# A complex-decay linear attention and a softplus layer on one core: paced loads, low halves by identity products, 48-column key-value products, a new plan

## The chip, the cores and the metric
One core of a Trainium2 chip runs the whole program. The metric is the device time of one execution in microseconds (us); lower is better.

## The reference, cut to what matters
Batch 4, 8 heads, 768 steps, head width 48; tokens of width 384 go through a layer of inner width 2048.

```python
scale = np.minimum(mag, 0.999) / (mag + 1e-06)      # mag = |a|, complex decay per step and row
for t in range(S):
    new_re = ar * S_re - ai * S_im
    new_im = ar * S_im + ai * S_re
    S_re, S_im = (new_re + einsum('bhd,bhe->bhde', k[:, :, t], v[:, :, t]), new_im)
    y[:, :, t] = einsum('bhd,bhde->bhe', q[:, :, t], S_re)
x = y.transpose(0, 2, 1, 3).reshape(B * S, H * D)
h = x @ w_in                                         # (3072, 384) @ (384, 2048)
g = np.maximum(h, 0.0) + np.log1p(np.exp(-np.abs(h)))
out = g @ w_out                                      # (2048, 384)
```

## The kernel before, in words
The steps are cut into 24 chunks of 128 steps of one batch. Four chunks, one of each batch, make a group of 512 tokens, so there are six groups. For the first group each chunk is a slice of its own (four slices); later slices hold two chunks.

For a slice, `pre` turns the decay into running sums of its logarithm and of its angle and multiplies q and k by the resulting exponentials, sines and cosines (VectorE and ScalarE, some 20 instructions a slice; for the first group the running sums are TensorE products with a triangle, L583). The last two steps, L654 and L656, are the slice's tail. `chunk` then moves the turned q and k into another layout by four DMAs from SBUF to SBUF (L702, L706; tile `qk`), multiplies them (scores, L748), masks them (L752), multiplies with v (L784, tile `y`) and, from the second group on, adds the state's part (L781). It also transposes k (L721) and adds the key-value products to the state (L810), which need the tiles `v` and `vo`. The tokens `y` go into `xt` as a high half (L793) and a low half (L794), so that products of float32r tiles keep float32's precision: three such products, high by high, high by low and low by high, stand for one.

`moe` runs the layer for a group: for each of 16 f blocks nine products into `h` (L846), the softplus on ScalarE and VectorE, and nine products into three accumulators `o` (L882); in the first group the second product takes w_out as plain float32 (L879, three products a block). The weights arrive as pairs of 32-bit words in eight blocks each of w_in and w_out (L388, 768 KB a load). VectorE puts the words together (L398, L401, L405); for a w_in block ScalarE then rounds the high half (L412) and VectorE subtracts it for the low half (L415).

All instructions are tasks of a planner. It simulates the five engines and one DMA server with the costs written at each task and with keys from a table `K`, and so fixes the order of each engine. On the chip, each engine runs its list in order and waits on semaphores. SP issues all loads and moves, so a DMA that waits holds back all that stand behind it. Where the simulated TensorE has nothing to do ahead of the layer's first second product, the planner puts filler products in its list (L908, results unused).

## Time and profile before

| | us |
|---|---|
| median of three runs | 579.37 (579.27 to 582.35) |
| the profiled execution | 580.82 |
| its span, first to last instruction | 579.1 |
| TensorE busy | 551.1 |
| VectorE busy | 430.9 |
| ScalarE busy | 426.8 |
| first of the layer's products (L846) starts at | 66.33 |

Read it from both ends. TensorE is busy for nearly the whole span, yet until the layer starts a part of that is filler. So the profile has two parts: a head, up to some 66 to 72 us, in which the first group's tokens are made, and a long rest in which the products of the layer follow each other with the later groups' attention between them. A float32 product appears as two instructions in the trace. Names of engines in rows: PE is TensorE, DVE is VectorE, ACT is ScalarE, SPq is the queue of SyncE.

### The profile page before, as it was taken

What the parts mean: (1) busy time and instruction counts of PE and PEld (TensorE: products, weight loads), DVE (VectorE), ACT (ScalarE), POOL (GpSimd) and SP (SyncE); (2) the same over time, 40 slices, a digit from 0 to 9 for tenths busy, and PEclk for the clock granted to TensorE, in tenths of its full rate; (3) what the DMA queues carried; (4) which work ended last, traced back from release to release, by engine and by line L of the source; (5) the groups of instructions that cost most, each with busy time, mean ns of one, the idle gap of its engine ahead of it and who ended that gap; (6) DMA issues with size and microseconds to landing.
All of it is one profiled execution on the core that took longest, in us unless ns stands there. A gap on an engine that the chain in (4) does not pass through costs nothing.

```text
span 579.1 us, 14114 instructions
## 1 busy us (share of the span) xinstructions
PE 551.1 (95%) x5952; PEld 439.9 (76%) x5952; DVE 430.9 (74%) x669; ACT 426.8 (74%) x756; POOL 3.8 (1%) x23
## 2 busy tenths in 40 slices
PE   0998899999999999999999999999999999999995
PEld 0997766576677888888888888888888878888883
DVE  6696899999897999988688767776966543544442
ACT  7972597868589798785977847958949899854442
POOL 2000000000000000000000000000000000000000
PEclk9998999999999999999999999999999999999998
DMA  8879920162644414464251532412247975120002
GB/s 316 351 213 278 406 96 0 35 184 58 164 148 110 141 33 103 149 166 142 65 168 48 118 125 70 117 35 102 69 126 236 306 236 184 42 55 0 1 0 60
DMA packets 44262, 76.09 MB, mean 131 GB/s; under 512 B 3744, under 2 KB 29344, under 8 KB 44192
## 3 DMA queue, kind: packets, MB, share of 16 engines
q1 hardware_dynamic: 44192, 75.12, 42.7%
q8 instruction: 48, 0.79, 0.6%
q14 instruction: 22, 0.18, 0.1%
HBM read 51.51 MB, written 4.72 MB: 97 GB/s over the span
## 4 chain that ended last, share of the span: by engine, by line
PE 82%; ACT 7%; DVE 4%; DMA 3%; issue 2%; SPq 0%; ACTq 0%; DVEq 0%
PE h L846 31%; PE o L882 25%; PE o L879 7%; PE att L748 4%; PE o L908 3%; PE att L810 3%; PE att L781 3%; PE att L784 2%; PE att L721 2%; ACT seen L460 1%; DMA seen<-w_in_dram 1%; DMA x<-dense_dram 1%; ACT lt L852 1%; ACT seen L459 1%; DMA seen<-w_out_dram 1%
## 5 line engine op out<-in xcount | busy, mean ns | idle before, releaser
L846 PE MATMUL h<-xt,wi 128*128 128x512 f32 x864 | 220.1, 402 | 1.5 <-DVE lt L862 1.2
L846 PEld LDWEIGHTS h<-xt,wi 128*128 128x128 f32 x864 | 159.6, 188 | 42.6 <-issue 2.9
L882 PE MATMUL o<-gh,wo 128*128 128x512 f32 x480 | 161.3, 397 | 0.0
L862 DVE SCALAR_TENSOR_TENSOR lt<-h,lt 128x512 f32<-128x512 f32 x80 | 54.6, 689 | 97.4 <-ACT lt L853 96.8
L882 PEld LDWEIGHTS o<-gh,wo 128*128 128x128 f32 x480 | 90.1, 188 | 21.1 <-issue 0.6
L851 ACT ACTIVATE lt<-h 128x512 f32<-128x512 f32 x96 | 56.2, 594 | 67.2 <-PE h L846 62.8
L882 PE MATMUL o<-gl,wo 128*128 128x512 f32 x240 | 94.1, 392 | 0.0
L853 ACT ACTIVATE lt<-lt,fixed 128x512 f32<-128x512 f32 x96 | 68.5, 721 | 1.5
L852 ACT ACTIVATE lt<-lt 128x512 f32<-128x512 f32 x96 | 59.9, 632 | 1.6
L866 DVE TENSOR_TENSOR gl<-lt,gh 128x512 fp32r<-128x512 f32 x80 | 54.6, 689 | 3.7 <-ACT gh L865 1.2
L882 PEld LDWEIGHTS o<-gl,wo 128*128 128x128 f32 x240 | 45.1, 188 | 9.7 <-DVE gl L866 0.2
L879 PE MATMUL o<-gf,raw_wo 128*128 128x512 f32 x96 | 43.5, 594 | 0.0
L966 ACT ACT_TABLE_LOAD x30 | 38.5, 1283 | 0.5
L562 DVE TENSOR_TENSOR_SCAN t<-hold,t 128x384 f32<-128x384 uint8 x40 | 36.1, 945 | 0.7
L752 DVE TENSOR_TENSOR a<-att,mask 128x512 f32<-128x512 f32 x48 | 31.4, 684 | 6.7 <-PE att L748 3.8
L748 PE MATMUL att<-qk 96*32 96x96 f32 (+3 forms) x1536 | 33.5, 236 | 1.9 <-issue 1.9
L748 PEld LDWEIGHTS att<-qk 96*32 96x32 f32 x1536 | 30.3, 111 | 6.1 <-issue 4.5
L879 PEld LDWEIGHTS o<-gf,raw_wo 128*128 128x128 f32 x96 | 17.9, 190 | 17.7 <-issue 16.3
L908 PE MATMUL o<-ident 128*128 128x128 f32 x198 | 27.6, 293 | 0.0
L908 PEld LDWEIGHTS o<-ident 128*128 128x128 f32 x198 | 25.6, 206 | 0.9 <-issue 0.6
L864 DVE TENSOR_SCALAR gh<-lt 128x512 fp32r<-128x512 f32 x52 | 22.0, 425 | 3.7
L865 ACT ACTIVATE gh<-lt 128x512 fp32r<-128x512 f32 x28 | 17.2, 626 | 8.7 <-DVE lt L862 8.6
(95 smaller groups left out, 694.4 us busy)
## 6 DMA issues: line engine op xcount, KB each, us to landing
x<-dense_dram SPq DMA_DIRECT2D x20, 768.0 KB, 5.8
qk<-x SPq DMA_DIRECT2D x48, 288.0 KB, 4.2
raw_wo<-w_out_dram SPq DMA_DIRECT2D x8, 768.0 KB, 8.1
raw_wi<-w_in_dram SPq DMA_DIRECT2D x8, 768.0 KB, 10.3
seen<-w_in_dram SPq DMA_DIRECT2D x16, 384.0 KB, 4.2
seen<-w_out_dram SPq DMA_DIRECT2D x16, 384.0 KB, 4.9
v<-vpad_dram SPq DMA_DIRECT2D x24, 224.0 KB, 2.8
qk<-x SPq DMA_DIRECT2D x48, 96.0 KB, 3.7
```

Of the source, the lines that this page charges most:

```text
L562: V.tensor_tensor_scan(out()[:, s], self.hold, inc()[:, s], 0.0, ALU.mult, ALU.add)
L748: PE.matmul(psc()[QT * u : QT * (u + 1), hh * P + f : (hh + 1) * P], q[:, h, CH + f : CH + f + QT], q[:, h, f:CH], start=True, stop=True)
L846: PE.matmul(h()[:, :n], w()[:, q, i, fs], xt()[:, x, i], start=k == 0, stop=k == 3 * NI - 1)
L851: add("ACT", a1(n) - 0.04, lambda: A.activation(tv(), h(), AF.Abs), k, r=[h], w=[t])
L852: add("ACT", a1(n), lambda: A.activation(tv(), tv(), AF.Exp, scale=-1.0), k, w=[t], tab="log")
L853: add("ACT", a1(n, 1), lambda: A.activation(tv(), tv(), AF.Ln, bias=self.one), k, w=[t], tab="log")
L862: add("DVE", d1(n), lambda: V.scalar_tensor_tensor(tv(), h(), 0.0, tv(), ALU.max, ALU.add), k, r=[h], w=[t])
L866: add("DVE", d1(n), lambda: V.tensor_tensor(gl(), tv(), gh().bitcast(F32), ALU.subtract), k, r=[t, gh], w=[gl])
L879: PE.matmul(acc[m]()[:, :n], v, gt[0](), start=f == 0, stop=f == NF - 1)
L882: PE.matmul(acc[m]()[:, :n], w()[:, wq, f % 2, ms], x(), start=f == 0 and q == 0, stop=f == NF - 1 and q == 2)
L908: self.nc.tensor.matmul(self.acc0[0]()[:, :P], self.ident, x, start=True, stop=True)
L966: nc.scalar.preload_act_table_set(TABLES[table])
```

## The change
1. Loads of weights, x, v and vo that the plan starts after 10 us get one more wait: for the ScalarE or VectorE instruction that, in the plan, was the last to end before the load's start.
2. The low halves of w_in blocks 0 to 3 are made by TensorE: identity times the value (float32) plus a negated identity times the high half, in two pieces of 384 columns, in PSUM; ScalarE or VectorE copies each piece out. Before, VectorE subtracted (L415).
3. The first group's tokens get their low half by one product of the negated identity with the high half, added onto `y` in PSUM, and a copy. Before, VectorE subtracted (L794). The negated identity lies in the room of w_out block 4.
4. The key-value products of even heads have 48 columns where they had 64; copies and additions of the state have 384 columns where they had 448. GpSimd clears the four states at the start.
5. Three in ten of each run of fillers, all but the first runs, are left out. ScalarE may take the sign step of the angle (L621). The planner's DMA server is faster for loads (400 KB per us after 0.5, where it was 330 after 0.65) and slower for the moves of q and k; a transpose costs 0.32 where it cost 0.25. All keys in `K` are new, so the whole order is new.

The diff, without the table `K` and with some bookkeeping left out (the loads of x, v and vo get `.pace = True` as the weight load does; `minus` is the negated identity):

```diff
+NLOW = 4
 NAT = {"i": 0, "o": 8}
 FILL = 0.2233
+KEEP = 0.7
+PACED = 10.0
...
                 if e == "SP":
-                    dma_free = max(dma_free, now + dur + 0.65) + t.nbytes / 330e3
-                    t.end = dma_free + 2.0
+                    dma_free = max(dma_free, now + dur + 0.5) + t.nbytes / 400e3
+                    t.end = dma_free + 1.7
...
-        return out
+        return self.thin(out)
+
+    def thin(self, out):
+        runs, run = [], []
+        for t in out:
+            if t.eng == "PE":
+                if t.idx < 0:
+                    run.append(t)
+                elif run:
+                    runs.append(run)
+                    run = []
+        drop = set()
+        for run in runs:
+            if run[0].start > runs[0][0].start + 2 * self.WIN:
+                drop.update(run[math.ceil(KEEP * len(run)) :])
+        return [t for t in out if t not in drop]
...
+        minus = self.minus = Buf(self.wpool, f"wo{TRIB - 1}", [P, 2 * NI * WCOL], F32R, "minus")
...
+        for sp in self.state:
+            add("POOL", 0.5, lambda sp=sp: G.memset(sp(), 0.0), -1e5, w=[sp])
...
+        add("DVE", 0.2, lambda: V.tensor_scalar(minus()[:, :P], self.ident, -1.0, None, ALU.mult), -1e5, w=[minus])
...
-            add("SP", 0.45, load, k - K["rlead"], w=[raw], nbytes=n * self.wwords * 4 * P)
+            add("SP", 0.45, load, k - K["rlead"], w=[raw], nbytes=n * self.wwords * 4 * P).pace = True
...
-                add("DVE", d1(n), lambda: V.tensor_tensor(
-                    flat(fin, 1), bits()[:, :n].bitcast(F32), flat(fin, 0).bitcast(F32), ALU.subtract),
-                    k, r=[bits, (fin, 0)], w=[(fin, 1)])
+                if kind == "o" or b >= NLOW:
...
+                    return
+                for z in range(2):
+                    ps = Buf(self.ps, "h", [P, 512], F32, f"low{b}_{z}", 2)
+                    h = slice(z * n // 2, (z + 1) * n // 2)
+
+                    def differ(ps=ps, h=h):
+                        nc.tensor.matmul(ps()[:, : n // 2], self.ident, bits()[:, h].bitcast(F32), start=True, stop=False)
+                        nc.tensor.matmul(ps()[:, : n // 2], self.minus()[:, :P], flat(fin, 0)[:, h], start=False, stop=True)
+
+                    add("PE", 0.86, differ, k, r=[bits, (fin, 0), self.minus], w=[ps])
+                    x = add("ACT", a1(n // 2), lambda ps=ps, h=h: A.activation(flat(fin, 1)[:, h], ps()[:, : n // 2], AF.Copy),
+                            k, r=[ps], w=[(fin, 1)])
+                    x.alt["DVE"] = (d1(n // 2), lambda ps=ps, h=h: V.tensor_copy(flat(fin, 1)[:, h], ps()[:, : n // 2]))
...
         def fold():
-            add("DVE", d2(W), lambda: V.tensor_scalar(
+            x = add("DVE", d2(W), lambda: V.tensor_scalar(
...
+            x.alt["ACT"] = (a1(W), lambda: A.activation(v4(), v3(), AF.Abs))
...
-        add("DVE", d1(DM), lambda: V.tensor_tensor(
-            xt()[:, 1, :, off : off + CH], y3(), hi().bitcast(F32), ALU.subtract),
-            at(), r=[y, (xt, (gc, 0))], w=[(xt, (gc, 1))])
+        lo = lambda: xt()[:, 1, :, off : off + CH]
+        if first:
+            add("PE", 0.19, lambda: PE.matmul(y3(), self.minus()[:, :P], hi(), start=False, stop=True, skip_group_check=True), at(), r=[(xt, (gc, 0)), self.minus], w=[y])
+            x = add("ACT", a1(DM) - 0.05, lambda: A.activation(lo(), y3(), AF.Copy), at(), r=[y], w=[(xt, (gc, 1))])
+            x.alt["DVE"] = (d1(DM), lambda: V.tensor_copy(lo(), y3()))
...
-                    s = slice(c0, c0 + (D if h % 2 else VP - D))
+                    s = slice(c0, c0 + D)
...
+            def reals(t):
+                a = t()[: 2 * D, :VW]
+                return bass.AP(a.tensor, a.offset, [a.ap[0], (VP, H // 2), (VP - D, 2), (1, D)])
...
+            done = []
             for t in self.plan.order(lambda: self.filler(self.ident), self.opener, self.gate):
...
                 t.fn()
+                ins = nc.cur_bb.bb.instructions[-1]
+                if t.eng in ("ACT", "DVE"):
+                    done.append((t.end, ins))
+                elif t.pace and t.start > PACED:
+                    after = max((x for x in done[-60:] if x[0] <= t.start), key=lambda x: x[0])
+                    self.tc.add_manual_dep(ins, after[1].name, mybir.DependencyInfo(
+                        mybir.DependencyClass.Sync, mybir.DependencyReason.DATA), reason="pace")
```

## Rows read from the trace of the kernel before

**Rows 1.** Page part 1: busy time, share of the span and instructions of each engine.
```profile
PE 551.1 (95%) x5952; PEld 439.9 (76%) x5952; DVE 430.9 (74%) x669; ACT 426.8 (74%) x756; POOL 3.8 (1%) x23
```

**Rows 2.** Stages: length; busy time of each engine; clock granted; DMA share; GB/s.
```profile
30.00:46.00 16.00, 16.00 (x365) 14.96 (x363) 15.33 (x27) 12.64 (x27) 0.00 (x0) 1.00 0.86 236
46.00:66.30 20.30, 15.74 (x357) 14.46 (x357) 13.67 (x21) 4.50 (x7) 0.00 (x0) 0.92 0.99 332
...
72.00:140.00 68.00, 68.00 (x556) 44.16 (x555) 66.78 (x94) 54.01 (x87) 0.00 (x0) 1.00 0.25 76
...
440.00:480.00 40.00, 39.56 (x454) 32.15 (x453) 19.83 (x34) 36.70 (x88) 0.00 (x0) 1.00 0.83 253
```

**Rows 3.** Page part 5, the fillers: line, count, busy us, mean ns of one, idle before.
```profile
L908 PE MATMUL o<-ident 128*128 128x128 f32 x198 | 27.6, 293 | 0.0
```

**Rows 4.** Timeline of PE, 45 to 67 us: start, us, line, count, idle before.
```profile
48.71 0.25 PE L810 MATMUL att<-v,kt 128*32 128x64 f32 x3 [2.69 <-issue]
...
48.91 1.81 PE L748 MATMUL att<-qk 96*32 96x32 f32 x62
...
54.61 1.31 PE L748 MATMUL att<-qk 96*32 96x128 f32 x64
...
58.51 0.66 PE L748 MATMUL att<-qk 96*32 96x128 f32 x22
61.04 1.01 PE L748 MATMUL att<-qk 96*32 96x32 f32 x42 [1.87 <-issue]
61.98 1.83 PE L908 MATMUL o<-ident 128*128 128x128 f32 x14
63.73 1.08 PE L784 MATMUL y<-a,v 128*32 128x128 f32 x32
...
66.33 4.43 PE L846 MATMUL h<-xt,wi 128*128 128x512 f32 x18
```

**Rows 5.** Timeline of DVE, same stretch.
```profile
42.01 0.96 DVE L656 TENSOR_TENSOR x<-x,t 128x768 f32<-128x768 f32 x1
...
61.52 1.29 DVE L752 TENSOR_TENSOR a<-att,mask 128x512 f32<-128x512 f32 x2 [1.68 <-PE att L748]
```

**Rows 6.** DMA issues, median us to landing: 26 to 66, then 100 to 440.
```profile
raw_wi<-w_in_dram SPq DMA_DIRECT2D x5, 768.0 KB, 11.0
...
qk<-x SPq DMA_DIRECT2D x8, 288.0 KB, 7.5
...
v<-vpad_dram SPq DMA_DIRECT2D x3, 224.0 KB, 12.5
...
qk<-x SPq DMA_DIRECT2D x36, 288.0 KB, 4.1
v<-vpad_dram SPq DMA_DIRECT2D x17, 224.0 KB, 2.7
```

**Rows 7.** Waits of SP's queue, 0 to 80: us in total, times, longest.
```profile
SPq L702 <- DVE x L656: 14.5, 1, 14.5
```

**Rows 8.** DVE by line, 0 to 72; then ACT's tokens by line.
```profile
L415 DVE TENSOR_TENSOR wi<-bits_wi,wi 128x768 fp32r<-128x768 f32 x3 | 2.9, 950 | 0.0
L794 DVE TENSOR_TENSOR xt<-y,xt 128x384 fp32r<-128x384 f32 x4 | 2.2, 558 | 2.2 <-ACT xt L793 2.2
...
L793 ACT ACTIVATE xt<-y x4: 491/491/492, 42.6 to 64.9; 128x384 fp32r<-128x384 f32 x4
```

**Rows 9.** Chain of waits in order of time: start, us, line, count.
```profile
72.32 2.09 PE h L846 x9
74.41 2.57 PE o L879 x6
```

**Rows 10.** Timeline of PE: key-value products of one chunk.
```profile
31.16 0.29 PE L810 MATMUL att<-v,kt 128*32 128x64 f32 x6
31.27 0.26 PE L810 MATMUL att<-vo,kt 128*32 128x48 f32 x6
31.36 0.29 PE L810 MATMUL att<-v,kt 128*32 128x64 f32 x6
```

More of the change, by code (lines that the diff above doesn't have):

```diff
@@ L88 @@
 class Task:
-    __slots__ = ("eng", "dur", "fn", "key", "idx", "deps", "outs", "bufs", "tab", "nbytes", "left", "ready", "end", "alt", "mode")
+    __slots__ = ("eng", "dur", "fn", "key", "idx", "deps", "outs", "bufs", "tab", "nbytes", "left", "ready", "start", "end", "alt", "mode", "pace")
     def __init__(self, eng, dur, fn, key, idx, tab, nbytes, mode=0):
@@ L93, in __init__ @@
         self.eng, self.dur, self.fn, self.key, self.idx, self.tab, self.nbytes = eng, dur, fn, key, idx, tab, nbytes
-        self.deps, self.outs, self.bufs, self.end = set(), [], [], 0.0
+        self.deps, self.outs, self.bufs, self.start, self.end, self.pace = set(), [], [], 0.0, 0.0, False
         self.alt = {}
@@ L241, in order @@
                     t = Task("PE", FILL, filler, 0, -1, None, 0)
+                    t.start = now
                     free[e] = now + self.array(now, t.dur + (self.SWITCH[0] if mode else 0.0))
@@ L271, in order @@
                 free[e] = now + dur
-                t.end = now + dur
+                t.start, t.end = now, now + dur
                 if e == "SP":
-                    dma_free = max(dma_free, now + dur + 0.65) + t.nbytes / 330e3
-                    t.end = dma_free + 2.0
+                    dma_free = max(dma_free, now + dur + 0.5) + t.nbytes / 400e3
+                    t.end = dma_free + 1.7
                 ends.append((t.end, t))
@@ L527, in pre @@
                 region(j), self.dense[:, base + 2 * j * W : base + 2 * (j + 1) * W].rearrange("p (c n) -> p c n", c=m)),
-                k + 0.1 * j, w=w, nbytes=8 * W * P)
+                k + 0.1 * j, w=w, nbytes=8 * W * P).pace = True
         for c in range(m):
@@ L532, in pre @@
             add("SP", 0.45, lambda vt=vt, gc=gc: nc.sync.dma_start(vt()[:, :VW], self.vpad[:, gc, :VW]),
-                K["chunk"][gc] - K["vlead"], w=[vt], nbytes=4 * VW * P)
+                K["chunk"][gc] - K["vlead"], w=[vt], nbytes=4 * VW * P).pace = True
             if not last:
@@ L536, in pre @@
                 add("SP", 0.45, lambda vo=vo, gc=gc: nc.sync.dma_start(vo()[:, :VO], self.vpad[:, gc, VW:]),
-                    K["state"][gc] - K["vlead"], w=[vo], nbytes=4 * VO * P)
+                    K["state"][gc] - K["vlead"], w=[vo], nbytes=4 * VO * P).pace = True
         add("ACT", a1(W), lambda: A.activation(v1(), re(), AF.Ln), at(), r=ra, w=[t1], tab="log")
@@ L587, in sums, with keep @@
             return ps, v, t
-        def keep(j, c, ps, v, key):
+        def keep(j, c, ps, v, key, last=()):
             f = car[j]
@@ L592, in keep @@
             add("DVE", 0.07, lambda: V.tensor_copy(
-                f().rearrange("p (b i) -> p b i", b=2)[:, q], n3(v())[:, :, CH - 1]), key, r=[ps], w=[(f, q)])
+                f().rearrange("p (b i) -> p b i", b=2)[:, q], n3(v())[:, :, CH - 1]), key, r=[ps], w=[(f, q), *last])
         part = lambda z, c: z if first else (z, c)
@@ L605, in pre @@
                         at(), r=[lb], w=ca if first else [(x, (c, 0))], tab="log")
-                keep(0, c, lb, vl, at())
+                keep(0, c, lb, vl, at(), [lb])
         else:
@@ L709, in chunk @@
         for y in range(2):
-            add("SP", 0.62, lambda y=y: heads(y), at(), r=rs, w=[(room, y)], nbytes=2 * D * NI * 1024)
+            add("SP", 0.62, lambda y=y: heads(y), at(), r=rs, w=[(room, y)], nbytes=3 * D * NI * 1024)
         for y in range(2):
-            add("SP", 0.62 if y else 1.4, lambda y=y: shared(y), at(), r=rs, w=[(room, 2 + y)], nbytes=2 * D * 1024)
+            add("SP", 0.62 if y else 1.4, lambda y=y: shared(y), at(), r=rs, w=[(room, 2 + y)], nbytes=3 * D * 1024)
         if not last:
@@ L731, in evac @@
                                  p3[:, :, 2 * D :].rearrange("p i (y r) -> p i y r", y=2), AF.Copy)
-                add("PE", 0.25, trans, at("state"), r=[q for q in rs if q[1] != (zc, 1 - j)], w=[pst])
+                add("PE", 0.32, trans, at("state"), r=[q for q in rs if q[1] != (zc, 1 - j)], w=[pst])
                 add("ACT", 0.43, evac, at("state"), r=[pst], w=[(kt, j)])
@@ L771, in ymm @@
         def ymm():
-            yy, q, v = y(), qk(), vt()
+            yy, v = y(), vt()
             def o(G):
@@ L777, in ymm @@
             if not first:
-                s = sp()
+                s, q = sp(), qk()
                 for G, h, co, prim in sched:
@@ L785, in ymm @@
                           start=first and prim and G < 4, stop=not prim)
-        add("PE", 0.9 if first else 1.78, ymm, at(), r=[room, vt] + am + ([] if first else [sp]), w=[y], mode=1)
+        add("PE", 0.9 if first else 1.78, ymm, at(), r=[vt] + am + ([] if first else [room, sp]), w=[y], mode=1)
         off = b * CH
@@ L1172 @@
+        7019.775, 6367.468, -1885.414, 3338.459, 627.569, 6737.113,
     ],
     "moe": [
[L1174 removed]
+        48.696, 119.345, 228.067, 305.249, 451.499, 6921.054,
     ],
     "step": [
[L1177 removed]
+        4.749, 7.163, 4.63, 7.188, 17.603, 4004.219,
     ],
[L1179 to L1184 removed]
@@ L1185 @@
-    "mpen": 2.176,
-    "altpen": 0.035,
-    "tpen": 0.597,
+    "seen": 423.345,
+    "seenstep": 10.777,
+    "rlead": 308.396,
+    "xlead": -1254.94,
+    "vlead": -1611.951,
+    "backlog": 1.427,
+    "mpen": 5.895,
+    "altpen": 0.69,
+    "tpen": 9.883,
     "table": 1.3,
     "nudge": {
[28 rows of a table removed]
[136 rows of a table added]
     },
```

56 lines of the change are left out of this document (26 added, 30 removed), and 164 rows, old and new, of the table K.

## The prediction

> **What bounds the kernel now.** I read the page's first part, then the busy time by stages, and only then single engines. TensorE is busy 551.1 us of a span of 579.1 [rows 1], so 28.0 us are left as idle, and of the busy time 27.6 us are fillers that compute nothing [rows 3]. The other 523.5 us are work. A shorter run can therefore come from three places: from the 27.6 + 28.0 = 55.6 us that are no work, from fewer columns on TensorE, or from a clock that is higher where it is low.
>
> The stages say where the 55.6 us lie. From 72 to 140 us TensorE is busy throughout and VectorE 66.78 of 68 us; even in the busy stretch from 440 to 480 TensorE is idle only 0.44 us of 40 [rows 2]. All fillers, and nearly all idle time other than the drain at the end, lie ahead of the layer's first product at 66.33 us [rows 3, 4]. So the head is what can be shortened, and each microsecond by which the layer starts earlier shortens the run by one, as long as TensorE stays fed afterwards.
>
> What ends the head? The tail of the last of the four slices ends at 42.01 + 0.96 = 42.97 us [rows 5], yet the last scores end only at 61.04 + 1.01 = 62.05 [rows 4]. In between ScalarE is busy 4.50 of 20.3 us and VectorE 13.67, but the DMA engines 0.99 of their time [rows 2]. A move of q and k takes 7.5 us there against 4.1 later, a v load 12.5 against 2.7, and a w_in load 11.0 [rows 6]. So this stretch is one of transfers that stand in each other's way: weights wanted much later are carried beside moves wanted now. Two breaks show it: TensorE stops 2.69 us before a key-value product, and 1.87 us in the middle of one group of scores (22 instructions before, 42 after it) [rows 4]. The profile names no releaser for either; both lie in the stretch of full DMA engines, which is all that the rows say.
>
> **The change part by part.** The profiled execution took 580.82 us for its span of 579.1, 1.45 us above the median of 579.37. I sum against 580.82 and take 1.45 off at the end.
>
> *Pace and new order in the head.* The loads keep their bytes and number; they are issued later, so the moves of q and k and the v loads find freer engines. What the full engines cost on the way to the layer is the two breaks, 2.69 + 1.87 = 4.56 us, and the longer move of the last chunk, 7.5 - 4.1 = 3.4 us: together 8.0 us. The ends: nothing, if the engines turn out to bind; and at most what VectorE allows. It works 13.67 us in that stretch [rows 2], from which the change takes three L415 (2.9 us) and four L794 (2.2 us) [rows 8], leaving 8.6 us, so the layer can't start before 46 + 8.6 = 54.6, a gain of 11.7 us. (The bare chain allows a little more: 42.97 + 4.1 for the move, 1.31 scores, 1.29 mask, 1.08 y, 0.49 and 0.56 for the halves gives 51.8 [rows 4 to 6, 8].) I take 8.0, since VectorE ran 15.33 of 16 us in the stretch ahead [rows 2] and could fill the shorter one almost as densely. The added wait stands on SP: behind a held load queue the moves of q and k, for which the scores wait, and the next x and v loads, for which ScalarE's first step of a slice and the products with v wait. In the head that is the slower rival below. After it I price the wait at nothing, as the DMA engines are at 0.25 of their time from 72 to 140 us [rows 2] and loads land in 2.7 to 4.1 us [rows 6]; if that cover is gone, it is the +4.6 of the rest below.
>
> *Fewer fillers.* A run of 14 fillers takes 1.75 us (61.98 to 63.73) [rows 4]. The mask for the last y ends at 61.52 + 1.29 = 62.81 [rows 5], so y starts 0.9 us late behind fillers. Three in ten of 14 are 0.5 us, and there is one such run before y and one before the layer: a gain of 1.0, between 0 and 1.8 (both waits wholly).
>
> *Low halves of w_in.* Nine float32r products of 512 columns take 2.09 us, 0.232 each; six instructions, three float32 products, take 2.57 us, 0.857 each [rows 9]. Two pieces of 384 columns are three quarters of that: 0.643 + 0.174 = 0.82 us each, and eight pieces make 6.5 us more on TensorE. What lies under fillers costs nothing; what comes after the layer's start costs in full. Three L415 lay before 72 us [rows 8] with the start at 66.33; with a start 8 us earlier I put two blocks in the head and two after it: 3.3 us, ends 0 and 6.5. The eight copies (like L793, 0.49 us for 384 columns [rows 8]) go to ScalarE, which has 15.8 us free between 46 and 66; if it has none, VectorE gets them back and its relief is gone.
>
> *Low half of the tokens.* Four products of 0.174 us, three under fillers; the last chunk's path gets 0.17 + 0.49 us in place of 0.56: +0.1.
>
> *Key-value products.* A 64-column group takes 31.27 - 31.16 = 0.11 us to the next, a 48-column one 0.09 [rows 10]. Four heads of each of 16 chunks after the head: 4 x 16 x 0.02 = -1.3 us; the first four chunks' share is under fillers. The smaller copies of the state save some 0.05 us of an engine off the path each. Clearing the states on GpSimd, the negated identity on VectorE (0.2 us by the planner) and the sign step on ScalarE lie beside other work and count for nothing; without that cover they would be some tenths at the start.
>
> *The rest of the order.* From 72 us on there is little to win: I take 0, from -0.4 (the idle time of the one stretch shown) to +4.6 (the two breaks over again at another place).
>
> Sum: -8.0 - 1.0 + 3.3 + 0.1 - 1.3 = -6.9, so 573.9 for an execution like the profiled one, and 572.5 for the median.
>
> **The rivals.** *The head is shorter still* (0.14). VectorE's bound is met and all low halves find room under fillers: -11.7 - 1.0 + 0.1 - 1.3 = -13.9, so 565.5. For it: ScalarE is mostly idle there. Against: the low halves need fillers that a short head no longer has.
>
> *The engines bind* (0.16). The transfers are hidden anyway: VectorE, which is nearly full before 46 and after 72 us [rows 2], sets when the words of w_in and w_out are ready, and the layer, started early, waits for them. Then 2 us of the 8.0 stay and the low halves are paid: -2.0 + 3.3 + 0.1 - 1.3 = +0.1, so 579.5, the same. For it: 66.78 of 68 us. Against: the change relieves just this engine.
>
> *The clock falls* (0.06). After the break of 2.69 us, 62 score instructions took 1.81 us where 64 took 1.31 [rows 4], and the granted clock is 0.92 of 2.4 GHz over the stretch [rows 2], so part of it ran at 1.2. With three in ten fillers gone the gaps are longer. If the last scores (1.31), y (1.08) and the first 18 products of the layer (4.43) ran at half clock, that is 6.8 us, and -6.9 becomes 579.3. Against: the runs keep seven in ten. The Trainium skill speaks against this part of the change: "TensorE: Matmul & The Clock Gate", "HAM oscillation", says that an array left idle too long falls back to half its clock and the next burst starts slow, and advises to keep it busy. The trace agrees in that one place.
>
> *The pace holds back the moves* (0.14), the slower end. SP works strictly in order: before, it once waited 14.5 us for the first tail [rows 7] with all loads behind it. If a held load ahead of a move waits for an instruction that runs later on the chip than in the plan, the moves behind it are late, and with them the weights; transfers that fill 0.99 of the stretch [rows 2] can't catch up. A w_in load takes 11.0 us where a fresh v load takes 2.7 [rows 6], so one weight load late by 8 us undoes the gain of 8.0 and adds as much again: +8.0 - 1.0 + 3.3 + 0.1 - 1.3 = +9.1, so 588.5. The point from which it decides is a delay of 8.0 + 2.9 = some 10 us of the last move against my forecast. The load of w_out block 4 is the likeliest place, since it waits until the negated identity is no longer read.
>
> **How the numbers follow.** The forecast has 0.50, its own range 567 to 577; the rivals 0.14, 0.16, 0.06 and 0.14. A difference under 0.5%, 2.9 us, can't be told from none here. Faster: 0.50 + 0.14 and a small part of the two near 579.4, together 0.67; same: 0.19; slower: 0.14. For 8 in 10 the range reaches from 563.5, below which half of the first rival lies at most, to 583, above which the slower one lies: it leaves out some 0.17.
>
> **What would show it.** Right: the first product of the layer at 58 to 59 us, moves of q and k landing in under 5.5 us, no break inside a group of scores, L415 four times fewer, two blocks' low halves ahead of the first layer product. Wrong: a DMA share still near 1 up to the layer's start, SP waiting long on ScalarE or VectorE ahead of a move, low halves mostly after the start, gaps of TensorE between 60 and 140 us, or a granted clock under 0.9 in the head.

## The result, and the profile after

The changed kernel takes 583.08 us in the median of 20 runs (580.83 to 586.34), the kernel before, run beside it on the same chip, 579.98 us. The ratio is 1.0054, with a 95% interval of 1.0034 to 1.0075: slower by half a per cent, where 572.5 us and faster was forecast. 583.08 also lies just above the range's upper end of 583.0.

The profiled execution of the changed kernel took 585.01 us for a span of 583.3, so it lies 1.9 us above its own median. That will matter: the two largest losses that it shows are not those of the median.

Line numbers moved: products of the layer are L892, L928 and L925 now (L846, L882, L879 before), scores L786 (L748), y L822 (L784), key-value products L853 (L810), transposes L759 (L721), fillers L954 (L908), moves of q and k L740 and L744 (L702, L706), the tail L694 (L656), loads of weights L411, of x L563, of v and vo L569 and L573. New are the low halves by products: L448 (float32) and L449 (float32r) for w_in, L834 for the tokens. L489 loads words of the weights a second time, for a check of their size on ScalarE (tile `seen`, L496, L497); it was there before, at L452, and I had not counted it.

The page of after, its first part and the queues of part 3 (packets, megabytes, share of the 16 DMA engines):

```profile
PE 549.0 (94%) x5880; PEld 432.8 (74%) x5880; DVE 434.1 (74%) x685; ACT 421.0 (72%) x743; POOL 5.7 (1%) x27
...
q1 hardware_dynamic: 44192, 75.12, 42.8%
q8 instruction: 48, 0.79, 0.6%
```

TensorE's busy time did shrink by 2.1 us [rows 1], and fillers went from 27.6 us [rows 3] to 13.3; yet the span grew by 4.2. Now the head. The timeline of PE in after, as in [rows 4]:

```profile
44.36 0.25 PE L853 MATMUL att<-vo,kt 128*32 128x48 f32 x3
46.75 0.23 PE L853 MATMUL att<-vo,kt 128*32 128x48 f32 x2 [2.14 <-issue]
...
55.66 2.13 PE L786 MATMUL att<-qk 96*32 96x128 f32 x107
58.87 0.59 PE L786 MATMUL att<-qk 96*32 96x64 f32 x19 [1.07 <-issue]
...
61.15 0.81 PE L448 MATMUL low<-bits_wi,ident 128*128 128x384 f32 x2
...
62.15 0.81 PE L448 MATMUL low<-bits_wi,ident 128*128 128x384 f32 x2
...
63.06 1.08 PE L822 MATMUL y<-a,v 128*32 128x128 f32 x32
...
65.89 1.32 PE L892 MATMUL h<-xt,wi 128*128 128x512 f32 x4
```

The layer starts at 65.89 us, 0.44 earlier than before [rows 4], where 58 to 59 was forecast. Both breaks are still there, again inside a group of key-value products and inside a group of scores. All eight pieces of the low halves lie ahead of the layer (from 47.29 us on; the last two are shown). The transfers, from the DMA issues between 26 and 66 us (count, KB each, median us to landing), to be read against [rows 6]:

```profile
raw_wi<-w_in_dram SPq DMA_DIRECT2D x3, 768.0 KB, 6.2
qk<-x SPq DMA_DIRECT2D x8, 288.0 KB, 7.2
...
v<-vpad_dram SPq DMA_DIRECT2D x2, 224.0 KB, 4.2
```

The loads land sooner (6.2 for 11.0, 4.2 for 12.5), the moves, for which the scores wait, do not (7.2 for 7.5). And SP's timeline shows when the last moves were issued. The last four go out at 48.56 us and later, 9.4 us and more after the last tail had ended (at 39.14 us, before at 42.97 [rows 5]):

```profile
42.02 1.23 SPq L740 DMA_DIRECT2D qk<-x  x2
43.29 1.45 SPq L744 DMA_DIRECT2D qk<-x  x1
47.43 0.39 SPq L489 DMA_DIRECT2D seen<-w_in_dram  x1
47.87 0.59 SPq L744 DMA_DIRECT2D qk<-x  x1
48.56 1.12 SPq L740 DMA_DIRECT2D qk<-x  x1
49.72 2.06 SPq L744 DMA_DIRECT2D qk<-x  x2
51.83 0.61 SPq L740 DMA_DIRECT2D qk<-x  x1
```

SP's waits in after, from 0 to 100 us (us in total, times, longest; the queue's answer to [rows 7]), say what stood there. The first row is the moves' own wait for the tails; below it are loads held for VectorE and ScalarE, as the change wants it, and a check load (L489) held for a key-value product.

```profile
SPq L740 <- DVE x L694: 27.6, 3, 25.7
SPq L569 <- DVE bits_wo L421: 7.3, 1, 7.3
SPq L563 <- ACT wi L452: 2.7, 1, 2.7
SPq L411 <- DVE t L669: 2.7, 2, 2.4
SPq L489 <- PE att L853: 2.6, 1, 2.6
```

Behind the head, two stretches of after answer to [rows 2] (columns as there) and one is new:

```profile
72.00:140.00 68.00, 67.81 (x580) 43.54 (x583) 55.18 (x76) 54.06 (x84) 0.00 (x0) 1.00 0.27 83
440.00:480.00 40.00, 39.82 (x189) 31.98 (x180) 21.51 (x35) 35.36 (x77) 0.00 (x0) 1.00 0.75 218
476.00:500.00 24.00, 21.74 (x309) 17.15 (x308) 10.40 (x18) 17.13 (x39) 0.00 (x0) 0.86 0.38 108
```

The middle is as dense as before, with VectorE relieved (55.18 us for 66.78). From 476 to 500 us there is a loss. PE's timeline there:

```profile
480.64 0.69 PE L786 MATMUL att<-qk 96*32 96x128 f32 x24
483.59 1.72 PE L786 MATMUL att<-qk 96*32 96x32 f32 x40 [2.26 <-DMA qk<-x]
485.24 4.21 PE L892 MATMUL h<-xt,wi 128*128 128x512 f32 x9
```

A late move costs 2.26 us, and then the granted clock is half for 6.8 us: nine products take 4.21 us where they take 2.09 at full clock [rows 9]. Together that is some 5.7 us (2.26 and half of 6.8). It looks like the whole answer. The experiments say that it is not.

### The profile page after: what moved, and what is told of

It reads as the page before. It is cut to its first block, busy times and chain, and to the rows that moved or that the text cites. A ratio compares the mean times of both kernels' runs of the same rounds, so it can differ in the third digit from the quotient of the medians.

```text
span 583.3 us, 14001 instructions
## 1 busy us (share of the span) xinstructions
PE 549.0 (94%) x5880; PEld 432.8 (74%) x5880; DVE 434.1 (74%) x685; ACT 421.0 (72%) x743; POOL 5.7 (1%) x27
## 4 chain that ended last, share of the span: by engine, by line
PE 81%; DMA 7%; ACT 6%; DVE 2%; issue 2%; SPq 1%; ACTq 0%; DVEq 0%
PE h L892 32%; PE o L928 25%; PE o L925 7%; PE att L786 5%; PE att L819 3%; PE att L822 3%; DMA qk<-x 3%; PE att L853 2%; DMA seen<-w_out_dram 2%; PE att L759 2%; DMA x<-dense_dram 1%; ACT seen L497 1%; PE low L448 1%; ACT L1013 1%; ACT seen L496 1%
## 5 line engine op out<-in xcount | busy, mean ns | idle before, releaser
L892 PE MATMUL h<-xt,wi 128*128 128x512 f32 x864 | 222.8, 405 | 1.3 <-DVE lt L908 1.3
L892 PEld LDWEIGHTS h<-xt,wi 128*128 128x128 f32 x864 | 161.2, 190 | 43.0 <-issue 3.7
L928 PE MATMUL o<-gh,wo 128*128 128x512 f32 x480 | 161.1, 396 | 0.0
L908 DVE SCALAR_TENSOR_TENSOR lt<-h,lt 128x512 f32<-128x512 f32 x80 | 54.6, 688 | 77.6 <-ACT lt L899 77.3
L928 PEld LDWEIGHTS o<-gh,wo 128*128 128x128 f32 x480 | 90.2, 188 | 21.7 <-issue 1.2
L928 PE MATMUL o<-gl,wo 128*128 128x512 f32 x240 | 94.2, 392 | 0.0
L928 PEld LDWEIGHTS o<-gl,wo 128*128 128x128 f32 x240 | 45.1, 188 | 9.7
L925 PE MATMUL o<-gf,raw_wo 128*128 128x512 f32 x96 | 44.1, 597 | 0.0
L910 DVE TENSOR_SCALAR gh<-lt 128x512 fp32r<-128x512 f32 x79 | 33.5, 424 | 10.0 <-PE o L928 7.0
L786 PE MATMUL att<-qk 96*32 96x32 f32 (+3 forms) x1536 | 33.7, 237 | 4.1 <-DMA qk<-x 2.9
L786 PEld LDWEIGHTS att<-qk 96*32 96x32 f32 x1536 | 30.1, 111 | 7.9 <-issue 3.8
L925 PEld LDWEIGHTS o<-gf,raw_wo 128*128 128x128 f32 x96 | 17.6, 190 | 16.6 <-issue 15.5
L766 ACT ACTIVATE kt<-att 128x288 f32<-128x288 f32 x40 | 17.7, 443 | 15.9 <-PE att L759 14.9
L692 DVE TENSOR_TENSOR x<-x,t 128x768 f32<-128x768 f32 x24 | 22.0, 953 | 9.5 <-ACT t L654 9.5
L620 PE MATMUL sum<-tri,t 128*128 128x128 f32 x48 | 9.9, 376 | 19.5 <-ACT t L651 17.1
```

What stands on the lines that cost most here:

```text
L786: PE.matmul(psc()[QT * u : QT * (u + 1), hh * P + f : (hh + 1) * P], q[:, h, CH + f : CH + f + QT], q[:, h, f:CH], start=True, stop=True)
L892: PE.matmul(h()[:, :n], w()[:, q, i, fs], xt()[:, x, i], start=k == 0, stop=k == 3 * NI - 1)
L908: add("DVE", d1(n), lambda: V.scalar_tensor_tensor(tv(), h(), 0.0, tv(), ALU.max, ALU.add), k, r=[h], w=[t])
L910: x = add("DVE", d2(n), lambda: V.tensor_scalar(gh(), tv(), 1.0, None, ALU.mult), k, r=[t], w=[gh])
L925: PE.matmul(acc[m]()[:, :n], v, gt[0](), start=f == 0, stop=f == NF - 1)
L928: PE.matmul(acc[m]()[:, :n], w()[:, wq, f % 2, ms], x(), start=f == 0 and q == 0, stop=f == NF - 1 and q == 2)
```

## The experiments

Each ratio is to the kernel before, run on the same chip beside it (medians 580.99, 580.46, 580.69, 580.36 and 581.32 us in the five sets). A difference of two ratios carries both intervals, so one under some 0.35% can't be told from none.

| kernel | median, us | ratio | 95% |
|---|---|---|---|
| the change | 583.08 | 1.0054 | 1.0034 to 1.0075 |
| a_nopace: no waits on loads | 579.63 | 0.9988 | 0.9963 to 1.0014 |
| e_head: waits ahead of 100 us alone | 583.40 | 1.0051 | 1.0025 to 1.0077 |
| e_late: waits behind 100 us alone | 580.91 | 0.9999 | 0.9976 to 1.0022 |
| e_weights: waits on large loads (weights, x) | 583.01 | 1.0056 | 1.0029 to 1.0083 |
| f_wts: waits on weights alone | 583.11 | 1.0039 | 1.0018 to 1.0061 |
| f_x: waits on x alone | 582.75 | 1.0039 | 1.0016 to 1.0061 |
| f_seen: first check load behind the moves | 582.17 | 1.0022 | 0.9998 to 1.0046 |
| a_seen: check loads issued by GpSimd | 583.73 | 1.0046 | 1.0029 to 1.0063 |
| b_seen: the same in the kernel before | 581.24 | 1.0013 | 0.9994 to 1.0032 |
| n_after: no check of the weights | 581.27 | 1.0008 | 0.9992 to 1.0024 |
| n_nopace: no check, no waits | 579.47 | 0.9964 | 0.9941 to 0.9988 |
| n_before: the kernel before, no check | 579.63 | 0.9982 | 0.9959 to 1.0006 |
| c_nopace_low: no waits, low halves on VectorE | 582.94 | 1.0049 | 1.0022 to 1.0075 |
| c_nopace_keep: no waits, all fillers | 580.24 | 0.9998 | 0.9969 to 1.0027 |
| d_kv64: no waits, 64-column products | 581.25 | 1.0017 | 0.9992 to 1.0043 |
| a_shift: 32 fillers more at the start | 583.82 | 1.0055 | 1.0030 to 1.0080 |

### Do the waits cost, and where?

*a_nopace* takes the waits away; the order of each engine stays.

```diff
-                elif t.pace and t.start > PACED:
+                elif False:
```

> The changed kernel without the added waits on loads (the order of SP stays). Theory P: the waits hold back what stands behind them on SP; without them the layer starts 2 us earlier or more and the time falls by 3 us or more, to 580 or less. Theory Q: the waits are not what holds the moves; the layer starts within 1 us of 65.9 and the time stays within 582 to 584.5. A third outcome: without the waits loads run ahead again and the moves of q and k land later than 7.2 us, 585 or more: then the pace is worth what it was meant for, and something else ate it.

Measured: 0.9988, so the waits cost 0.66% (1.0054 - 0.9988), some 3.8 us. Without them the change can't be told from the kernel before; with them it is a loss. In its profile the break near 480 us is 0.60 us long and the clock stays whole. From these two profiles I took it that the loss lay there, at the last chunk. The next two runs put that to the test.

*e_head* and *e_late* keep the waits on one side of 100 us of the plan.

```diff
-                elif t.pace and t.start > PACED:
+                elif t.pace and PACED < t.start < 100.0:   # e_head
+                elif t.pace and t.start > 100.0:           # e_late
```

> The change with its waits on loads kept only for loads that the plan starts before 100 us; order and computation as in the change. So far: all waits 1.0054 of the kernel before, no wait 0.9988. Theory L (most of the waits' 3.8 us come from late loads: the break ahead of the last scores and the half clock behind it): 1.001 or less, 580 to 581 us, no fall of the clock near 483 us. Theory H (most of it comes from the head, where loads held back delay the moves and the layer's start): 1.004 or more, 582.5 to 583.5 us, with the first product of the layer 1 us or more later than without waits.

> The counterpart: waits only for loads that the plan starts after 100 us. Theory L: 1.004 to 1.006, 582.5 to 583.7 us, break and half clock near 480 us as in the change. Theory H: 1.001 or less, at most 581 us. If neither half alone costs, the two act on each other: a late start of the layer moves the last chunk's moves to where they hurt.

Measured: 1.0051 with the early waits alone, 0.9999 with the late ones alone. All of the loss that can be told comes from the head, and theory L, my own, falls. In e_late the break in the last scores is 0.40 us, although all late waits are there; in e_head it is 0.81 us without any of them; the clock stays whole in both. The long late break is not confined to one execution: *a_shift* below, which keeps all waits and the check as they are, has 1.71 us there and then half clock for 3.4 us. But early waits alone, without it, cost as much as all waits, so the half per cent of the median does not need it and lies elsewhere.

Where, the stretches show (columns as in [rows 2]; the last but one is the DMA engines' share). First after, then e_head, then e_late:

```profile
17.00:38.00 21.00, 18.44 (x167) 17.39 (x168) 20.43 (x40) 19.99 (x38) 0.00 (x0) 1.00 1.00 356
38.00:46.00 8.00, 5.89 (x183) 4.88 (x182) 6.48 (x11) 3.16 (x8) 0.00 (x0) 1.00 1.05 258
```

```profile
17.00:38.00 21.00, 18.48 (x104) 17.68 (x104) 18.60 (x37) 17.68 (x33) 0.00 (x0) 1.00 0.99 351
38.00:46.00 8.00, 8.00 (x246) 7.42 (x245) 7.07 (x11) 5.54 (x15) 0.00 (x0) 1.00 0.96 241
```

```profile
17.00:38.00 21.00, 16.46 (x153) 15.69 (x154) 19.58 (x39) 18.82 (x35) 0.00 (x0) 0.92 1.03 374
38.00:46.00 8.00, 8.00 (x225) 7.28 (x225) 7.23 (x11) 4.95 (x13) 0.00 (x0) 1.00 0.78 199
```

A load that is held at 20 to 38 us is not saved, it is carried later. With waits 356 and 351 GB/s move until 38 us, without 374; the difference, 18 to 23 GB/s over 21 us, is 0.4 to 0.5 MB. From 38 to 46 us, when the moves of the third and the fourth chunk are wanted, it comes back: 241 to 258 GB/s for 199, and a DMA share of 0.96 to 1.05 for 0.78. In this stretch the profiles with waits on head loads have 0.96 to 1.06 (after, e_head, e_weights, f_wts, f_x, f_seen, a_seen, n_after), those without 0.69 to 0.78 (e_late, a_nopace, n_nopace, c_nopace_low, d_kv64); c_nopace_keep, without waits but with more fillers, lies between, at 0.89. SP's timeline of e_late, against that of after above:

```profile
42.30 1.23 SPq L740 DMA_DIRECT2D qk<-x  x2
43.57 1.41 SPq L744 DMA_DIRECT2D qk<-x  x1
45.32 0.39 SPq L489 DMA_DIRECT2D seen<-w_in_dram  x1
45.76 0.59 SPq L744 DMA_DIRECT2D qk<-x  x1
46.45 0.58 SPq L740 DMA_DIRECT2D qk<-x  x1
47.08 1.96 SPq L744 DMA_DIRECT2D qk<-x  x2
49.08 0.65 SPq L740 DMA_DIRECT2D qk<-x  x1
```

The last move is issued at 49.08 us without early waits, at 51.83 (after) and 52.10 (e_head) with them, and the layer of e_head starts at 68.05 us, of e_late at 65.34: 2.7 us later, where the medians differ by 0.52%, 3.0 us. (A single profile scatters: after itself starts at 65.89, e_weights at 65.06. The medians carry the verdict, the profiles the mechanism. Behind the layer's start the profiles of a_nopace, n_nopace, n_after and of all e and f runs last 511.1 to 514.1 us, with early waits or without; after lasts 517.4, with its late break.)

*e_weights*, *f_wts* and *f_x* ask which loads; *f_wts* and *f_x* strike `.pace = True` at all loads but those named in the table, *e_weights* adds a condition on the load's size (over 300 KB).

> Waits only on loads of over 300 KB (the 16 weight loads and the x loads of the later slices), none on the small v and vo loads. If it is the large loads whose issue is held, the time is that of the change, 1.005, 583 us. If it is the small v and vo loads whose wait holds SP's queue ahead of the moves, the time is that without waits, 0.999, 579.6 us.

> Waits only on the 16 loads of the weights, none on x, v and vo. If holding the weights back is what costs, 1.004 or more, 582.5 us and over; if the x loads are (ScalarE's first step of a slice waits for them), 1.001 or less, 581 us or below.

> The counterpart: waits only on the loads of x. The weights theory gives 1.001 or less, the x theory 1.004 or more. Both near 1.003 would say that the cost is the sum of small delays of either kind.

Measured: 1.0056, 1.0039 and 1.0039. The small loads of v and vo do not matter. Weights or x alone cost 0.5% each over no waits (0.9988), both together 0.66 to 0.68%. So neither of the two is the culprit, and they do not add up as two costs would: to hold either kind is enough. The last moves go out at 50.91 us in f_wts and at 53.93 in f_x, against 49.35 in a_nopace.

*f_seen* leaves all waits and puts the check load, which stands between the moves in SP's order, behind the last of them (`sp[i]`), and its two ScalarE steps (`use`) later too.

```diff
...
+        place = out.index(sp[i]) + 1
+        out.insert(place, seen)
+        place = max(place + 1, min(place + 60, out.index(nxt)))
+        out[place:place] = use
```

> The change with all its waits, but the first load of the weights' check, which stands in SP's queue ahead of five of the last moves of q and k, is put behind them, and its two ScalarE steps some later. In the profile of e_head it is issued at 47.40 us, in e_late at 45.32, and the last move follows at 52.1 against 49.1 us. Theory S (the waits cost because this load, held until the key-value products are done, holds the last chunk's moves): the last move some 2 us or more earlier, ratio 1.001 or less. Theory W (the moves only follow what is late anyway: the weights and products ahead of them): the ratio stays at 1.004 to 1.006, whenever the moves are issued.

Measured: 1.0022, between the two theories, and its interval touches both. The last move does go out at 49.75 us, 2 us sooner, as theory S says; but in its profile the break among the key-value products is still there (1.95 us) and the layer starts at 66.67. A part of the loss may hang on this place in the queue; how much stays open.

### The check of the weights

I first took the check's loads for the whole cause. *a_seen* and *b_seen* have GpSimd issue them, in the changed kernel and in the one before.

```diff
-                self.nc.sync.dma_start(raw().rearrange(...), src.bitcast(I32))
+                self.nc.gpsimd.dma_start(raw().rearrange(...), src.bitcast(I32))
```

> The changed kernel with one edit: the 32 loads of the weights' check (tile seen) are issued by GpSimd, not by SP; plan, order and all else stay. Theory Q (SP's queue): two of these loads stand ahead of moves of q and k in SP's order and wait there for room, once at 47 us and several times from 463 to 478 us. So the 2.26 us break ahead of the last chunk's scores goes, and with it 6.83 us at half clock, that is 2.26 + 3.4 = 5.7 us: median 575 to 578.5, no wait of L786 for a DMA, granted clock 1.00 from 476 to 500. Theory P (the pace itself holds the moves): nothing changes at either place, 582 to 584. If GpSimd issues slowly, ScalarE waits for seen and the time is above 584.

> The kernel before with the same edit: the 32 loads of the check are issued by GpSimd. Theory Q: there the moves of the last chunks were issued by 453.5 us with the first loads of the check between them, and TensorE waited nowhere for them, so the time stays within 0.3% of 580. If it falls by 3 us or more, the gain of the same edit on the changed kernel is one of GpSimd's queue in general and not of the place of the last moves.

Measured: 1.0046 and 1.0013. In a_seen the break near 480 us is gone and so is the fall of the clock there, yet the time is hardly less: the layer starts at 67.01 us, and the span lasts 7.7 us beyond the last step of VectorE, for 5.9 in after. That was the first sign that the late break was not the loss. As moving the loads to another engine has a price of its own, the next three leave the check out (its loads and its ScalarE steps; GpSimd sets its sums to zero). A held load that had waited for one of these steps then waits for the step ahead of it.

```diff
-                self.nc.sync.dma_start(raw().rearrange(...), src.bitcast(I32))
+                pass        # and the two ScalarE steps on the tile are left out
```

> The changed kernel, pace kept, that leaves out the check of the weights' high words: its 32 loads (tile seen) and their 64 ScalarE steps are not there, the plan and the order of all else are. Nothing then stands between the last chunks' moves on SP, and ScalarE has 44 us less to do. Theory Q (the changed kernel lost its time at the last moves, where these loads stand): 576 to 578.5, no break at 480 us. Theory P (the waits cost along the run): 580 or more.

> The same without the check and without the waits on loads. Against n_after it prices the waits where the weak place at the last moves is gone from both. Theory Q: within 1.5 us of n_after. Theory P: 3 us or more faster than n_after. In the profiles of both kernels with the check the waits had cost 1.2 us up to 480 us and the rest of 5.9 us after it, so I expect 575 to 577.5.

> The kernel before without the check of the weights' high words. TensorE waited for nothing there, so 579 to 581, as with the check. Against n_nopace it prices the new products together with the new order, without the weak place: if n_nopace is 2 to 4 us faster, the change has a gain that the last moves ate; if they are equal, it has none.

Measured: 1.0008, 0.9964 and 0.9982. The check costs 0.46% in the change with its waits (1.0054 - 1.0008), 0.24% without them and 0.18% in the kernel before; the last two are within what can't be told from none. And the waits cost 0.44% (1.0008 - 0.9964) where there is no check at all. So the waits cost without the check too. Whether the check makes them dearer (0.66 for 0.44%) can't be told from these intervals.

*c_sp* and *c_sp_nopace* had all check loads moved behind the moves in SP's order.

> The changed kernel, pace kept, with the loads of the check moved behind the moves of q and k in SP's order, wherever the plan starts such a move within 8 us; the one in the head (47 us) goes behind the first group's last move, its two ScalarE steps later too. This is the test of theory Q without GpSimd, whose queue added 2 us at the end of the run a_seen and disturbed its head. Theory Q (the break ahead of the last chunk's scores and the half clock after it are what the change lost): 576 to 579, no break over 0.5 us at 480 us. Theory P (the waits cost by themselves, along the whole run): 580.5 to 583, though the break at 480 us is gone.

> The same order of SP, and no waits on loads. Against c_sp it prices the waits alone, with the weak place at the last moves gone from both. Theory Q: the same as c_sp within 1.5 us, since a wait late by half a microsecond mattered only at that place. Theory P: 3 us faster than c_sp. Either way this should be the fastest of the family, 574 to 578, under the kernel before by 0.4% or more; if it is no faster than 579, the last moves were not what was lost.

My edit put a check's sum ahead of the step that it sums, so both programs took their general path (13,203 us) and their times say nothing. The fast part in their traces shows one thing: there is no break near 480 us, and ScalarE waited up to 3.9 us (c_sp) and 4.2 us (c_sp_nopace) for check loads that now came late. f_seen is the part of this edit that could be asked cleanly.

### The parts of the arithmetic

All without waits, against a_nopace (0.9988). *c_nopace_low* gives the low halves of w_in blocks 0 to 3 back to VectorE, at the same places of the order.

```diff
-                        nc.tensor.matmul(ps()[:, : n // 2], self.ident, bits()[:, h].bitcast(F32), start=True, stop=False)
-                        nc.tensor.matmul(ps()[:, : n // 2], self.minus()[:, :P], flat(fin, 0)[:, h], start=False, stop=True)
+                        V.tensor_tensor(flat(fin, 1)[:, h], bits()[:, h].bitcast(F32), flat(fin, 0)[:, h].bitcast(F32), ALU.subtract)
```

> The changed kernel without waits on loads and with the low halves of w_in blocks 0 to 3 made by VectorE again, each piece of 384 columns subtracted at the place in the order where TensorE's two products stood; the copies are left out. Against a_nopace (579.6) it prices the identity products. My prediction put half of them (3.3 us) behind the layer's start; the trace of the changed kernel has all eight ahead of it (47 to 63 us), two of them directly ahead of the last y. If they cost, 576 to 578.5; if they are hidden, 578.5 to 581; if VectorE's relief is worth more than they cost, 581 to 584.

Measured: 1.0049, slower by 0.61% (some 3.5 us), and the layer starts at 67.33 us for 65.62. The products are worth their price under this plan, which is made for them. Two things go with it in the profile of c_nopace_low: TensorE waits 3.14 and 0.87 us for VectorE's masks ahead of two y products, which have no such waits in a_nopace, and the granted clock over 46 to 66 us is 0.83 for 1.00, with half clock from 51.2 to 58.0 us. How much of the 3.5 us is VectorE's load and how much the clock that fell behind its waits, this run does not separate.

*c_nopace_keep* sets `KEEP = 1.0`.

> The changed kernel without waits on loads and with all fillers kept. Against a_nopace (579.6) it prices the thinning. My prediction: the thinning is worth 1.0 us, so 580 to 581.5 here. The rival by the clock: with all fillers the half clock in the head (3.4 us from 27.2 us in a_nopace) goes, and the time is 577 to 579.5. Also, more fillers move every later instruction, so breaks stand at other work but again at indices that are 193 plus a multiple of 256, as in all traces so far.

Measured: 0.9998, 0.1% more, which is none that can be told.

*d_kv64* goes back to 64 columns in the even heads' products.

```diff
-                    s = slice(c0, c0 + D)
+                    s = slice(c0, c0 + (D if h % 2 else VP - D))
```

> The changed kernel without waits on loads and with key-value products of 64 columns on the even heads again. Against a_nopace (579.6) it prices the 48 columns: my prediction had 1.3 us, from 0.02 us a group, so 580.5 to 581.5.

Measured: 1.0017, 0.29% or 1.7 us more than a_nopace. That fits the 1.3 us of the prediction, but the intervals overlap, so it is not shown to differ from none.

### What the breaks are

Counted from 0 in TensorE's records (weight loads, products and the 40 steps of its sequencer), the two breaks of before come ahead of numbers 961 and 1473, those of after ahead of 705 and 1217: always a multiple of 256 apart, whatever work stands there. *a_shift* puts 32 fillers, 128 records, at the start of TensorE's list. If a transfer of data is missing, the breaks stay with their work; if they belong to the place in the instruction stream, they stay at their numbers.

```diff
             done = []
+            for _ in range(32):
+                self.filler(self.ident)
```

> The changed kernel with 32 more filler products at the very start of TensorE's list, 128 instructions (a load of weights and a product, each twice), which run while TensorE has nothing else to do. It tests the two breaks inside groups (44.40 to 46.75 and 57.60 to 58.86 us), which stand 512 TensorE instructions apart, as the two of the kernel before do, each with one 16 KB packet of instructions about as long ahead of its end. Theory F (instructions are fetched): the breaks come 128 instructions earlier in the program, so at other work, at the same index counted from the first instruction plus or minus 256. Theory T (full DMA engines stop the work): they stay at the same groups, 128 further in the index. Time within 2 us of the changed kernel's either way, 581 to 585.

Measured: the time is that of the change (1.0055), and the breaks come ahead of numbers 705 and 1473, now a transpose and a low half. The timeline of PE in a_shift, around them:

```profile
42.14 1.30 PE L786 MATMUL att<-qk 96*32 96x32 f32 x63
45.40 0.77 PE L759 MATMUL att<-ident,x 128*128 128x128 f32 x5 [1.96 <-issue]
...
63.29 0.48 PE L448 MATMUL low<-bits_wi,ident 128*128 128x384 f32 x1
64.34 0.59 PE L448 MATMUL low<-bits_wi,ident 128*128 128x384 f32 x1 [0.56 <-issue]
```

They are breaks of the instruction stream. The page's queue q8, named instruction, carries 48 packets and 0.79 MB, 16 KB each; one of them starts 2.3 to 2.7 us ahead of each break's end, in before at 46.05 and 58.67 us, in after at 44.02 and 56.58.

The packets also say when a break comes. Numbering them from 0, packet n belongs to record 193 + 256 (n + 1), which in no profile of the kernels in the table, nor in that of before, starts sooner than 2.18 us after it. In the head the packet itself often starts late, with the DMA engines full. In after the packet for 705 starts 4.3 us behind record 449, with the engines at 1.02 in between; in a_nopace 1.2 us behind it, with the engines at 0.81, and TensorE passes 705 without a break. In before the packet for 705 starts at 35.78 us, well ahead of 705 at 41.61; the one for 961 starts 4.4 us behind 705, with the engines at 1.01, and there is the break. So breaks and full engines seem to belong together after all, by way of the instructions. This is read from the times of packets in the profiles; no run delays a packet by itself.

The break ahead of 705 then reaches the moves. The check load L489 goes out 0.06 to 0.08 us after the last key-value product of its chunk in each of after, e_late, a_nopace, e_head, e_weights, f_wts and f_x (in after 47.43 behind 47.36, in e_late 45.32 behind 45.24). So its wait of 2.6 us in after (0.3 in e_late) comes for the most part from the break of 2.14 us on TensorE, and the moves behind it on SP inherit it.

## Why the prediction was wrong

*What bounds the kernel.* That the head decides was right: e_head and e_late put the loss by the waits there. That the middle would not change was right too (67.81 of 68 us).

*Pace and new order, -8.0.* This is the step that failed, in both its parts. The 4.56 us of breaks were put down to full DMA engines "which is all that the rows say", and then booked as transfers of data that the pace would clear. They are waits for instructions, whose packets started late while the engines were full; the pace left them full, and after the change 2.14 and 1.07 us of breaks are there again. The 3.4 us for faster moves took it that held loads leave room. They do, earlier: loads landed in 6.2 us for 11.0. But the bytes came back between 38 and 46 us, and the moves took 7.2 us. Of the 8.0 us, the profiled executions show 0.44.

*The wait's price, 0.* The part says that behind a held load "the moves of q and k" wait, and then prices that at nothing but for one rival. It cost 0.66%, 3.8 us, and made a loss of a change that without it can't be told from none. Its cover, the DMA engines at 0.25 from 72 us on, was real (e_late 0.9999); for the head there was no such cover, and the term should have had a price from the first.

*The rival that the pace holds back the moves* was the right kind: SP in order, the last moves 2.7 us later (51.83 for 49.08), no time to catch up. Its place was wrong (w_out block 4; it was the large loads of the head, weights and x alike), and its size was 588.5 for a measured 583.08, since it adds a delay of 8.0 us where the waits cost 3.8.

*Fewer fillers, -1.0.* Nothing that can be told (c_nopace_keep). The reading was off too: not all fillers of before lie ahead of the layer's first product. The run ahead of it has 6 of them, and 14 (1.7 us) stand behind it, at 70.60 us. In after two low halves stand ahead of the last y (61.15 to 63.06) where the fillers had stood, so thinning has nothing to set free.

*Low halves, +3.3.* I expected two blocks behind the layer's start at full price; all eight pieces lie ahead of it. Taken back they cost 0.61%: under this plan a gain of some 3.5 us, not a cost. The relief of VectorE, which is busy 20.43 of 21 us from 17 to 38 us in after, entered only as a bound on the head term; it should have been a term, and with it the clock, which fell in c_nopace_low behind waits for VectorE.

*Key-value products, -1.3.* 1.7 us, of the size forecast, not told from none. *The tokens' low half* was not measured alone.

*The rest, 0, up to +4.6.* Without waits the change comes to 0.9988, 0.7 us less than before and not told from none, although two of its parts are priced at 3.5 and 1.7 us under its plan. If the two add up, some 4.5 us are lost elsewhere in the new order. This is a difference of terms and not shown by a run of its own; part of it may be that the plan was made with these parts in mind.

*The clock.* The rival with half clock in the head did not come about; the clock of after is whole there. It fell once, behind the 2.26 us break near 480 us, to half for 6.8 us. That agrees with the Trainium skill, "TensorE: Matmul & The Clock Gate", "HAM oscillation": an array that idles too long starts its next burst slow. In the median it is not what decides: e_head, at the ratio of all waits, has neither a break of that length nor a fall of the clock there. In the head the clock does fall in other profiles (granted over 46 to 66 us: 0.83 in f_x, 0.91 in e_head, f_wts and n_after), but also in two without waits (0.91 in n_nopace and d_kv64), so it does not part the two kinds.

Not settled: how much of the waits' cost is the check load's place in the queue (f_seen lies between), and whether the break ahead of record 705 carries the rest. It appears in seven profiles with early waits (after, e_head, e_weights, f_wts, f_x, f_seen, n_after: 0.58 to 3.77 us idle) and in none of a_nopace, e_late, n_nopace and d_kv64. But these have a longer break ahead of 1217 instead (1.73 to 2.72 us, for 1.07 in after), so the sum of the breaks does not part the two kinds: 2.23 us in e_head, 2.10 in a_nopace. And two kernels without waits have it as well, 0.88 us in c_nopace_keep and 0.64 in the fast part of c_sp_nopace, with the DMA engines at 0.89 and 0.94 from 38 to 46 us, and a_seen, with them, stops at 449 instead (2.24 us). What goes with the break ahead of 705 is thus full engines ahead of its packet, which early waits bring about and other plans can too.

## What to carry to other kernels

To hold a load back moves its bytes to a later time; before doing so, look at what is wanted then. Here the early DMA engines were full of things not yet needed, but the held loads met the moves that were. A break with no releaser in the profile must not be given the cause that suits the sum: move the work by some instructions and see whether the break stays with the work or with the place in the stream. And the largest loss of one profiled execution need not be that of the median; undo its cause before believing it.

## What the runs showed of the hardware

TensorE can stop at fixed places of its instruction stream, ahead of records 193 + 256 n. In the kernels here it does so only in the head, up to 64.3 us, and not at each of these places: the longest lasts 3.98 us from start to start (f_x, record 705). Where a break is over 0.3 us, the packet of the next block had started at most 2.95 us before its end (f_seen, record 449). Small products alone do not make a break: behind the head after uses up blocks of 256 records in 4.5 to 5.5 us as well (2241 at 121.98 and 2497 at 126.46 us, the packets 0.4 and 0.6 us behind records 2241 and 2497) and does not stop.

The Trainium skill, "Runtime: NRT & Kernel Launch", "Instruction fetch mechanics", gives these blocks their size, 16 KiB or 256 instructions, which agrees with the 48 packets of 16 KB (48 x 256 = 12,288 places for the 11,760 products and weight loads of after). It calls the cost of a boundary mostly hidden, and there the measurement decides: of four boundaries between 39 and 60 us in after, two cost 2.14 and 1.07 us of idle TensorE.
